# A gated recurrence and an FFT convolution: projecting all 256 channels at once, and shifts by half a period as signs in a second table

## The chip, the cores and the metric

One core of one Trainium2 chip runs the whole kernel. The metric is the time of one execution on the device in microseconds (us), as the median of several runs. One execution was also taken by the hardware profiler; all rows below come from that one.

## The reference

The input `x` has 4 batches of 6272 time steps and 256 channels. Two parts follow one another:

```python
sig = 1 / (1 + exp(-f_logit));  f = lower_bound + (1 - lower_bound) * sig
for t in range(S):                          # per batch and channel, S = 6272
    h = f[:, t] * h + (1 - f[:, t]) * x[:, t];  y[:, t] = h

x1, x2, x3 = split(y @ w_proj)              # 256 -> 3 * 256
X2 = rfft(x2, n=S, axis=1);  H = rfft(filter_fft, n=S, axis=0)
out = (x1 * irfft(X2 * H, n=S, axis=1) * x3) @ w_out
```

The convolution is circular over all 6272 steps, with one filter for each of the 256 channels.

## The kernel before

**The transform.** 6272 is 128 x 49, and these two have no common factor, so a transform of 6272 points becomes a transform of 128 points and one of 49, with no factors in between. Time index n is read as 128 q + 49 m, modulo 6272: for each of the 49 values of q (in the code `q_of(r)`), the 128 values of m are taken at a stride of 49 steps.

**The stages of a batch,** by the names in the code and the lines in the profile:

- `hgrn`: load `f_logit` and `x` in 13 pieces of 512 steps (`load`), sigmoid on ScalarE (`sig`, L353), the product on GpSimd (`u`, L355), transposes on TensorE (`sT` and `uT`, L362), the gate on ScalarE (`f`, L376) and the scan on VectorE (`scan`, L384). The scan writes h, in 16 bits, for two halves of 128 channels into the tile `HA`. For each piece GpSimd copies h once more past its end (`wrap`, L332), so that the stride of 49 can run over the end of the period: 100 copies in all.
- `phase_p` (`P`, L676): the projection to x2 and the gathering in one. The stationary operand is h at stride 49 (`HA[:, n0:n0 + Q * 127 + 1:Q]`), the moving operand 128 of the 256 columns of `W2`; two matmuls (the two halves of h's channels) for each r. It runs twice in a batch, for v = 0 and v = 1, since tile `X2` holds 128 channels; each time in 7 groups of 14 matmuls, and each group is copied out of PSUM into `X2` (`x2`, L327 on VectorE or L322 on ScalarE).
- `phase_f1` (`F1`, L690, evicted by `A`): the transform over 128 points, 8 pairs of channels in a unit, 16 units in a batch. `unit`: the transform over 49 points (`F2`, L738: four matmuls of 64 rows, two at a time in the upper and lower half of the array), the product with the filter's spectrum on VectorE (`prod`, L749), and the way back over 49 points (`I2`, L759, evicted by `Th`). `mini` (L711) and `zm` do the frequencies 0 and 64 of the 128 apart, with the filter's values in `Hm`.
- `gate`: x1 and x3 (`x13`, L412) are projected from h, evicted by ScalarE (`xs`, L424) and multiplied on GpSimd (`z`, L428) into `zt`.
- `phase_o`: the way back over 128 points (`I1`, L793), the product with `zt` (`y`, L799), the output projection (`proj`, L811), its eviction (`o`, L324) and the store.
- `prepare`, once: tables of sines, the weights, and the filter's spectrum (`rot`, `FF1`, `FF2`, L602, L619, L637), which goes to DRAM in 16 pieces (`hst`) and is loaded back in every batch (`H`).

**What sets the order.** The kernel records every operation with what it reads and writes. `Plan.schedule` then goes through a simulated time with costs for each operation, picks the next operation by start time and by priority (`LEAD` adds to priorities by kind and batch, `SHY` keeps kinds off engines), chooses the engine where there are two, and the PSUM banks (`room`: pairs of banks begin at an even bank). The instructions then stand on each engine in that order; on the chip an engine does not pass over an instruction that waits. Batches overlap: `hgrn` of the next batch runs beside the spectrum and the output stage of the present one. An operation of 64 rows (`ROWS`: F2, mini, I1, FF2, last) next to one of 128 rows makes TensorE change its mode.

**What waits for what around the change.** P needs all 26 pieces of h and all its copies past the end. The copies and the eviction buffer `A` of F1 lie in one part of `HA`. F1 needs all groups of `x2` of its half. P for v = 1 writes the same `X2` that F1 of v = 0 reads. `hgrn` of the next batch overwrites h, so it follows P for v = 1 and `x13`. Every `y` needs all 26 `z` of its batch.

Of the kernel before, what the change touches and what calls it, by code (L numbers as in the profile page):

```python
# [9 lines left out]
F32 = mybir.dt.float32  # L10
# [32 lines left out]
EW = 16384  # L43
AT = 6144
E0 = S - 176
E1 = S - 128


def q_of(r):

    return (18 * r) % Q
# [6 lines left out]
class Plan:  # L58
# [14 lines left out]
    SHY = {("A", "ACT"): 12, ("A", "DVE"): 31, ("Th", "ACT"): -13, ("Th", "DVE"): 637,  # L73
            ("afs", "ACT"): -3, ("afs", "DVE"): 28, ("f", "ACT"): -9, ("f", "DVE"): 18,
            ("f2", "ACT"): 978, ("f2", "DVE"): -356, ("fr", "ACT"): 65, ("fr", "DVE"): 449,
            ("fr", "POOL"): 310, ("hw", "ACT"): -51, ("hw", "DVE"): 109, ("o", "ACT"): -77,
            ("o", "DVE"): 1301, ("wrap", "ACT"): 636, ("wrap", "POOL"): 17, ("x2", "ACT"): 89,
            ("x2", "DVE"): 31}
# [6 lines left out]
        "A": (-75, 220, 598, 390), "F1": (561, 1834, 42, -2), "F2": (1153, -14, 2719, -82),  # L85
        "FF1": (861, 0, 0, 0), "FF2": (-3, 0, 0, 0), "H": (-41, -13, -344, -186),
        "I1": (-136, 778, -116, -26), "I2": (3, -264, 933, 15), "P": (1182, -300, 3, -112),
        "Th": (261, 84, -119, 0), "W": (3, 0, 0, 0), "f": (15, 14, 0, 0), "f2": (51, 0, 0, 0),
        "ff": (-67, 0, 0, 0), "fr": (1, 0, 0, 0), "hst": (146, 0, 0, 0), "hw": (622, 0, 0, 0),
        "last": (17, 0, 0, 0), "load": (-361, 63, 113, 165), "mini": (360, -626, -3, 39),  # L90
        "o": (-124, 109, 0, 37), "pre": (160, 0, 0, 0), "prod": (12, 0, -32, 135),
        "proj": (-1765, -5442, -1089, -504), "rot": (296, 0, 0, 0), "sT": (11, 7, 149, 755),
        "scan": (51, -58, -2, 148), "sig": (16, -225, 0, -421), "slot": (-4, 267, 15, 31),
        "store": (56, -11, -31, -3), "u": (12, -19, -7, -73), "uT": (1, -300, -798, -37),
        "warm": (-10, 0, 0, 0), "wrap": (505, -108, -107, -50), "x13": (0, -360, -13, -112),
        "x2": (1, 1, 50, 33), "xs": (251, 266, 157, 146), "y": (0, 101, -83, 11),
        "z": (-31, -259, -7, 5), "zm": (48, 300, -23, 414),
# [30 lines left out]
    @staticmethod  # L128
    def room(bank, n):

        best = None
        for b in range(0, 8, n):
            if None not in bank[b:b + n]:
                key = (max(bank[b:b + n]), n == 1 and bank[b ^ 1] is not None, b)
                if best is None or key < best:
                    best = key
        return best
# [108 lines left out]
def kernel(  # L246
# [24 lines left out]
    FT = konst.tile([128, 2, 128], F16, name="FT")  # L271
# [6 lines left out]
    Hm = konst.tile([128, 2, 2, 2, NEP], F16, name="Hm")  # L278


    HA = konst.tile([128, 2 * S + EW], F16, name="HA")
    A = HA[:, S + AT:S + AT + NA * UE * 128].rearrange("m (e r k) -> m e r k", r=2, k=64)
    HB = (0, S + EW)
# [4 lines left out]
    X2 = konst.tile([128, NEP // 2 * PW + 16], F16, name="X2")  # L288
# [16 lines left out]
    def E(a, z):  # L305

        return [("E", u) for u in range(a // 1024, (z - 1) // 1024 + 1)]
# [33 lines left out]
    def hgrn(b):  # L341
        for c in range(NCHK):
# [14 lines left out]
            for kh in range(2):  # L357
# [31 lines left out]
                a, o = (t0, t0) if kh == 0 else (max(t0, S - E1), EW - S + max(t0, S - E1))  # L389
                z = min(t0 + n, E0) if kh == 0 else t0 + n  # L390
                if z <= a:
                    continue
                op("wrap", {"POOL": 0.05 + (z - a) / 1015.0, "ACT": 0.08 + (z - a) / 1200.0},
                   lambda e, a=a, o=o, z=z, kh=kh: copy(
                       e, HA[:, S + o:S + o + z - a], HA[:, HB[kh] + a:HB[kh] + z]),
                   r=[("hn", kh, c)], w=E(o, o + z - a))
# [38 lines left out]
    def prepare(tmp):  # L435
        dve, pool, act = nc.vector, nc.gpsimd, nc.scalar
        at = (4096, 12288, 14336, 6144, 8192)
        raws = [(HA[:, S + a:S + a + 2048], E(a, a + 2048)) for a in at[:3]]
        raws += [(X2[:, i * 2048:(i + 1) * 2048], [("raw", i)]) for i in range(3)]
        raws += [(Hu[:, i].rearrange("m a e k -> m (a e k)"), [("Hu", i)]) for i in range(2)]  # L440
        raws += [(HA[:, S + a:S + a + 2048], E(a, a + 2048)) for a in at[3:]]
# [4 lines left out]
        def small(fn, n, r=(), w=(), e="DVE", k=1):  # L446
            op("pre", {e: k * (0.06 + n * (1.04e-3 if e == "DVE" else 1.5e-3))}, fn, r=r, w=w)

        op("pre", {"POOL": 1.0}, lambda e: make_identity(nc, iden), w=["iden"])
        rot = tmp.tile([128, 256], F32R, name="rot")  # L450
        for i in range(2):
            small(lambda e, i=i: dve.tensor_copy(rot[:, i * 128:(i + 1) * 128], iden[:]), 128,
                  r=["iden"], w=["rot"])
        op("pre", {"SP": 0.46}, lambda e: nc.sync.dma_start(
            wcol, lower_bound.rearrange("(a p) -> p a", p=128)), w=["wcol"], dma=0.3, lag=2.1)

        def oms(e):
# [4 lines left out]
        small(oms, 2, r=["wcol"], w=["om"], k=2)  # L462

        wp = HA[:, S:S + 3072].bitcast(F32).rearrange("p (k j) -> p k j", k=2)
        wo = HA[:, S + 3072:S + 4096].bitcast(F32).rearrange("p (k j) -> p k j", k=2)
        op("pre", {"SP": 0.46}, lambda e: nc.sync.dma_start(
            wp, moe_w_proj.rearrange("(a p) j -> p a j", p=128)), w=E(0, 3072), dma=2.1, lag=2.1)
        op("pre", {"SP": 0.46}, lambda e: nc.sync.dma_start(
            wo, moe_w_out.rearrange("(a p) j -> p a j", p=128)), w=E(3072, 4096), dma=0.8, lag=2.1)
        for kh in range(2):  # L470
# [4 lines left out]
               r=["om"] + E(0, 3072), w=["W13"])  # L475
            for p in range(2):
# [4 lines left out]
                   r=["om"] + E(0, 3072), w=["W2"])  # L481
        op("W", {"ACT": 0.5}, lambda e: act.copy(Wo[:], wo[:]), r=E(3072, 4096), w=["Wo"])


        scr, st = HA[:, S + 6144:S + 10240], E(6144, 10240)
# [5 lines left out]
        cols = tmp.tile([128, 9], F32, name="cols")  # L491
        kre, is0, kim, ore, oim, wt, k2, sgn, low = (cols[:, i:i + 1] for i in range(9))
        D1r = tmp.tile([128, 2, 128], F32R, name="D1r")
        FTr = tmp.tile([128, 2, TB], F32R, name="FTr")
# [4 lines left out]
        def iotas(e):  # L499
            pool.iota(pint, pattern=[[0, 1]], base=0, channel_multiplier=1)  # L500
            at = 0
            for n, pattern, base in (
                    (128, [[0, 2], [49, 64]], 0), (128, [[1568, 2], [0, 64]], 1568),
# [6 lines left out]
        small(iotas, 1260, r=["iden"], w=st + ["pint", "FT"], e="POOL")  # L510

        def args(e):
# [5 lines left out]
            stt(kim, in0=is0, scalar=64.0, in1=kre, op0=AOP.mult, op1=AOP.add)  # L518
# [19 lines left out]
            for i, (k, o) in enumerate(((kre, ore), (kim, oim))):  # L538
                ts(w[:, 520 + 256 * i:776 + 256 * i], in0=cI, scalar1=k, scalar2=o,
                   op0=AOP.mult, op1=AOP.add)  # L540

            big = 12582912.0
            ts(v, in0=w, scalar1=1.0 / S, scalar2=big, op0=AOP.mult, op1=AOP.add)
            ts(v, in0=v, scalar1=-big, scalar2=float(S), op0=AOP.add, op1=AOP.mult)
            dve.tensor_tensor(v, w, v, op=AOP.subtract)
        op("pre", {"DVE": 8.8}, args, r=st + ["pint", "rot"], w=["cols", "v"])
        op("pre", {"ACT": 0.97}, lambda e: act.activation(v, v, AF.Sin, scale=2.0 * math.pi / S),
# [3 lines left out]
            D1r[:], v[:, 0:128].unsqueeze(1).broadcast_to([128, 2, 128])), 256, r=["v"], w=["D1r"])  # L551
        for i in range(2):
            small(lambda e, i=i: dve.tensor_scalar(FTr[:, i], in0=tt[i], scalar1=low,
                                                   scalar2=None, op0=AOP.mult), 98, r=["v"],
                  w=["FTr"])

        def rest(e):
            pool.tensor_copy(D1[:], v[:, 0:128])
            for i in range(2):
                pool.tensor_scalar(FT[:, i, 0:98], in0=tt[i], scalar1=low, scalar2=None,  # L560
                                   op0=AOP.mult)
                pool.tensor_scalar(ID[:, i, :], in0=v[:, 520 + 256 * i:776 + 256 * i],
# [4 lines left out]
        op("pre", {"POOL": 3.9}, rest, r=["v", "FT"], w=["D1", "FT", "V", "ID"])  # L567
# [16 lines left out]
        small(gaps, 1920, r=["iden"], w=["f2e"], e="POOL")  # L584
# [3 lines left out]
        for g, r0 in enumerate(range(0, Q, 4)):  # L588
# [16 lines left out]
            for p in range(2):  # L605
# [4 lines left out]
                   w=[("f2", g, p)], src=rt)  # L610
        mX = tmp.tile([128, 2, NEP], F32R, name="mX")
        for u in range(NU):
            af = afs[:, u % 2]
            for h in range(2):
# [16 lines left out]
                w=["mX"], e="POOL")  # L631

            def second(e, pb, af=af):
                for r in range(2):
                    for e2 in range(2):
                        rows = slice(64 * e2, 64 * e2 + 64)
                        nc.tensor.matmul(PS[:TB, pb + e2, :], FTr[rows, r, :], af[rows, r],  # L637
# [11 lines left out]
        def last(e, pb):  # L649
            for k in range(2):  # L650
                for e2 in range(2):
                    rows = slice(64 * e2, 64 * e2 + 64)
                    nc.tensor.matmul(PS[:TB, pb + e2, k * NEP:(k + 1) * NEP], FTr[rows, k, :],
                                     mX[rows, k], start=True, stop=True)
        lst = op("last", {"PE": 0.3}, last, r=["mX", "FTr"], w=["FF2"], take=2)
        op("hw", either(512), lambda e, pb: copy(
            e, Hm[:TB, :, 0],
            PS[:TB, pb:pb + 2, 0:2 * NEP].rearrange("p a (k i) -> p a k i", k=2), HS),
           w=["Hm"], src=lst)
        for h in range(2):  # L660
            op("hst", {"SP": 0.36}, lambda e, h=h: nc.sync.dma_start(
# [226 lines left out]
```

## Time and profile before

| what | value |
|---|---|
| median of 3 runs | 520.24 us (518.5 to 520.66) |
| the profiled execution | 522.43 us, span of its instructions 520.6 us |
| clock granted to TensorE, mean | 0.984 |
| busy: TensorE, VectorE, ScalarE, GpSimd | 490.2, 440.3, 401.5, 394.5 us |
| DMA traffic | 116.53 MB |

PE is TensorE's matmuls, PEld its weight loads, DVE VectorE, ACT ScalarE, POOL GpSimd and SP the engine that issues the transfers. A busy time counts the union of an engine's instructions. Matmuls are pipelined: the mean duration of one is far longer than the time from the start of one to the start of the next, and the latter, called its pace below, is what a stream of them costs.

### The profile page before, as it was taken

What the parts mean: (1) busy time and instruction counts of PE and PEld (TensorE: products, weight loads), DVE (VectorE), ACT (ScalarE), POOL (GpSimd) and SP (SyncE); (2) the same over time, 40 slices, a digit from 0 to 9 for tenths busy, and PEclk for the clock granted to TensorE, in tenths of its full rate; (3) what the DMA queues carried; (4) which work ended last, traced back from release to release, by engine and by line L of the source; (5) the groups of instructions that cost most, each with busy time, mean ns of one, the idle gap of its engine ahead of it and who ended that gap; (6) DMA issues with size and microseconds to landing.
All of it is one profiled execution on the core that took longest, in us unless ns stands there. A gap on an engine that the chain in (4) does not pass through costs nothing.

```text
span 520.6 us, 13604 instructions
## 1 busy us (share of the span) xinstructions
PE 490.2 (94%) x5389; PEld 373.9 (72%) x5389; DVE 440.3 (85%) x464; ACT 401.5 (77%) x584; POOL 394.5 (76%) x363
## 2 busy tenths in 40 slices
PE   6989999999998999999999989999999999999796
PEld 5867777676655889687666879586677886585485
DVE  6899776898989798898998888998988998789764
ACT  5879797759986875768997864969998856869644
POOL 3576786949997987948999884949999957968800
PEclk9899999999998999999999999999999999999989
DMA  8978899434679899344879896444688951433157
GB/s 310 407 284 255 287 333 317 152 103 133 210 228 262 258 342 336 138 144 121 286 223 254 300 312 219 132 142 129 207 285 283 391 213 71 135 98 98 59 208 289
DMA packets 41938, 116.53 MB, mean 224 GB/s; under 512 B 4398, under 2 KB 6514, under 8 KB 41874
## 3 DMA queue, kind: packets, MB, share of 16 engines
q1 hardware_dynamic: 41874, 115.66, 65.7%
q8 instruction: 42, 0.69, 0.5%
q14 instruction: 22, 0.18, 0.1%
HBM read 84.54 MB, written 31.00 MB: 222 GB/s over the span
## 4 chain that ended last, share of the span: by engine, by line
PE 62%; DMA 15%; POOL 8%; ACT 7%; issue 3%; DVE 2%; SPq 0%; POOLq 0%; ACTq 0%; DVEq 0%
PE PS L412 13%; PE PS L362 11%; PE PS L676 9%; PE PS L811 8%; PE PS L759 7%; DMA FL<-in_f_logit_dram 6%; PE PS L738 5%; POOL zt L428 5%; PE PS L690 4%; DMA H<-Hu 4%; PE PS L793 4%; DMA XT<-in_x_dram 2%; POOL XT L355 2%; DMA HA<-in_moe_filter_fft_dram 2%; PE PS L619 1%
## 5 line engine op out<-in xcount | busy, mean ns | idle before, releaser
L428 POOL TENSOR_TENSOR zt<-x1s,x3s 128x490 f16<-128x490 f32 (+1 forms) x104 | 201.2, 1952 | 46.3 <-ACT x3s L424 34.3
L749 DVE TENSOR_TENSOR PP<-PS,Hu 98x1008 f16<-98x1008 f32 x128 | 146.6, 1198 | 13.1 <-PE PS L738 6.4
L355 POOL TENSOR_TENSOR XT<-XT,FL 128x1024 f32<-128x1024 f32 (+1 forms) x52 | 117.4, 2258 | 25.4 <-DMA XT<-in_x_dram 10.7
L384 DVE TENSOR_TENSOR_SCAN HA<-fTs,HA,PS 128x512 f16<-128x512 f32 (+1 forms) x96 | 113.9, 1204 | 14.2 <-PE PS L362 12.4
L412 PE MATMUL PS<-HA,W 128*128 128x490 f16 (+1 forms) x416 | 105.3, 370 | 3.4 <-ACT x1s L424 2.0
L324 ACT ACTIVATE osb<-PS 128x1024 f32<-128x1024 f32 (+1 forms) x52 | 50.7, 976 | 34.9 <-PE PS L811 33.8
L799 DVE TENSOR_TENSOR ys<-PS,zt 128x1024 fp32r<-128x1024 f32 (+1 forms) x52 | 59.9, 1156 | 20.0 <-PE PS L793 12.3
L376 ACT ACTIVATE fTs<-PS,nomc 128x512 f32<-128x512 f32 (+1 forms) x97 | 64.6, 667 | 11.8 <-PE PS L362 10.0
L424 ACT ACTIVATE x1s<-PS 128x490 f32<-128x490 f32 (+1 forms) x104 | 60.8, 585 | 12.3 <-POOL zt L428 7.6
L424 ACT ACTIVATE x3s<-PS 128x490 f32<-128x490 f32 (+1 forms) x104 | 61.1, 587 | 10.5 <-PE PS L412 10.4
L353 ACT ACTIVATE FL<-FL 128x1024 f32<-128x1024 f32 (+1 forms) x52 | 52.8, 1016 | 18.8 <-DMA FL<-in_f_logit_dram 18.8
L811 PE MATMUL PS<-Wo,ys 128*128 128x256 f32 x392 | 61.3, 299 | 4.3 <-DVE ys L799 2.2
L362 PE MATMUL PS<-iden,XT 128*128 128x128 f32 x392 | 62.2, 279 | 2.5 <-POOL XT L355 1.7
L362 PE MATMUL PS<-iden,FL 128*128 128x128 f32 x392 | 61.2, 277 | 2.8 <-ACT Th L322 2.4
L412 PEld LDWEIGHTS <-W 128*128 128x128 f16 x416 | 34.7, 98 | 39.9 <-issue 19.1
L332 POOL COPY HA<-HA 128x512 f16<-128x512 f16 (+2 forms) x100 | 56.2, 602 | 7.5 <-DVE HA L384 7.4
L759 PEld LDWEIGHTS <-PP 98*128 98x128 f16 x1024 | 50.4, 98 | 11.1 <-issue 3.6
L322 ACT CAST Th<-PS 128x784 f16<-128x784 f32 x64 | 52.8, 826 | 7.1 <-PE PS L759 6.9
L811 PEld LDWEIGHTS PS<-Wo,ys 128*128 128x128 f32 x392 | 51.7, 195 | 7.9 <-ACT osb L324 2.8
L759 PE MATMUL PS<-VA,PP 98*128 98x98 f16 x512 | 52.9, 208 | 2.2 <-POOL PP L741 1.2
L327 DVE CAST X<-PS 128x896 f16<-128x896 f32 x49 | 50.2, 1090 | 4.8 <-PE PS L676 4.6
L676 PEld LDWEIGHTS <-HA 128*128 128x128 f16 x784 | 52.6, 152 | 1.9 <-issue 0.6
(90 smaller groups left out, 694.1 us busy)
## 6 DMA issues: line engine op xcount, KB each, us to landing
Hu<-H SPq DMA_DIRECT2D x64, 392.0 KB
FL<-in_f_logit_dram SPq DMA_DIRECT2D x48, 512.0 KB
XT<-in_x_dram SPq DMA_DIRECT2D x48, 512.0 KB
out_dram<-osb SPq DMA_DIRECT2D x48, 512.0 KB
HA<-in_moe_filter_fft_dram SPq DMA_DIRECT2D x7, 512.0 KB
H<-Hu SPq DMA_DIRECT2D x16, 196.0 KB
H<-Hu SPq DMA_DIRECT2D x16, 128.0 KB
X<-in_moe_filter_fft_dram SPq DMA_DIRECT2D x3, 512.0 KB
```

The lines of the kernel that those rows point to most:

```text
L355: op("u", {"POOL": 0.1 + 0.553 * nb}, lambda e, xt=xt, ft=ft: nc.gpsimd.tensor_tensor(xt, xt, ft, op=AOP.mult), r=[("ft", k)], w=[("xt", k)])
L362: nc.tensor.transpose(PS[:, p, j:128 * nb:nb], src[:, j, cols], iden[:])
L376: nc.scalar.activation(fT, PS[:, p, 0:n], AF.Identity, scale=by, bias=1.0)
L384: nc.vector.tensor_tensor_scan(h, fT, PS[:, p, 0:n], init, op0=AOP.mult, op1=AOP.add),
L412: nc.tensor.matmul(PS[:, p, 0:n], W13[:, kh, js], HA[:, HB[kh] + t0:HB[kh] + t0 + n], start=(kh == 0), stop=(kh == 1))
L424: nc.scalar.activation(xs(i), PS[:, p, 0:n], AF.Copy, scale=1.0 if i else ZS),
L428: nc.gpsimd.tensor_tensor(late["zt"][:, jb, :, m0:m0 + nm], xs(0).rearrange("p (m r) -> p r m", r=Q), xs(1).rearrange("p (m r) -> p r m", ...
L676: nc.tensor.matmul(pp[:, r - 7 * g, :], HA[:, n0:n0 + Q * 127 + 1:Q], W2[:, kh, v * 128:v * 128 + 128], start=(kh == 0), stop=(kh == 1))
L749: nc.vector.tensor_tensor(PP[:TB, k, o, :, :, 1:64], px.unsqueeze(1).broadcast_to([TB, 2, UE, 63]), hh[:, :, :, 1:64], op=AOP.mult)
L759: nc.tensor.matmul(PS[:, ib + o, pr * TB:(pr + 1) * TB], PP[:TB, k, o, n, 2 * pr:2 * pr + 2, :], v[:TB], start=(n == 0), stop=(n == 1))
L799: nc.vector.tensor_tensor(late["ys"][:, yk, :, 0:rn * 128], PS[:, cb:cb + 2, 0:rn * 128], late["zt"][:].rearrange("p k r m -> p k (r m)") ...
L811: nc.tensor.matmul(po[:, i, :], late["ys"][:, yk, kh, i * 128:(i + 1) * 128], Wo[:, kh, :], start=(kh == 0), stop=(kh == 1))
```

## The change

1. `phase_p` runs once in a batch. Each matmul moves all 256 columns of `W2`; there are 98 in a batch in place of 196, in 13 groups. `X2` holds 256 channels.
2. Where q is over 24, the stationary operand starts half a period earlier (`- S // 2`). It then holds the same 128 values rotated by 64, and a rotation by half of 128 points changes only the sign of the odd frequencies. So `FT` gets a second table with these signs, F1's columns (`D1`) are ordered into 32 even and 32 odd frequencies, and each matmul of F2 becomes two of half its columns, one with each table: 8 matmuls of 256 columns in place of 4 of 512. `ID` follows the new order.
3. h is copied past its end for 3072 steps in both channel halves: 48 copies in place of 100. The copies and `A` have places of their own in `HA`.
4. `Hm` moves into the unused columns of `X2`; its second, rotated copy comes from four more small matmuls (`last`) in place of two transfers.
5. `room` lets pairs of banks begin at any bank. `LEAD` and `SHY` have other values, the kinds of `prepare` are told apart, and so the whole order is another.

```diff
-        for b in range(0, 8, n):
+        for b in range(9 - n):
...
-    HA = konst.tile([128, 2 * S + EW], F16, name="HA")
+    HA = konst.tile([128, 2 * (S + WR) + AW], F16, name="HA")
...
-    X2 = konst.tile([128, NEP // 2 * PW + 16], F16, name="X2")
+    X2 = konst.tile([128, NEP * PW + 16], F16, name="X2")
+    xv = X2[:, 0:NEP * PW].rearrange("m (i c) -> m i c", c=PW)
+    Hm = xv[:, :, Q:Q + 8].rearrange("m i (e a k) -> m e a k i", e=2, a=2)
...
-                a, o = (t0, t0) if kh == 0 else (max(t0, S - E1), EW - S + max(t0, S - E1))
-                z = min(t0 + n, E0) if kh == 0 else t0 + n
-                if z <= a:
+                z = min(t0 + n, WR)
+                if z <= t0:
                     continue
...
-                    (128, [[0, 2], [49, 64]], 0), (128, [[1568, 2], [0, 64]], 1568),
+                    (128, [[0, 2], [49, 2], [98, 32]], 0), (128, [[1568, 2], [0, 64]], 1568),
...
+                pool.tensor_scalar(FT[:, 1, i, 0:98], in0=FT[:, 0, i, 0:98], scalar1=odd,
+                                   scalar2=None, op0=AOP.mult)
...
-    def phase_p(b, v):
+    def column(t, q):
+        n0 = t + 128 * q - (S // 2 if q > Q // 2 else 0)
+        return HA[:, n0:n0 + Q * 127 + 1:Q]
+
+    def phase_p(b):
-        for g in range(7):
+        for g, r0 in enumerate(range(0, Q, 4)):
+            rn = min(4, Q - r0)
...
-                        n0 = HB[kh] + 128 * q_of(r) - (S if kh and r else 0)
-                        nc.tensor.matmul(pp[:, r - 7 * g, :], HA[:, n0:n0 + Q * 127 + 1:Q],
-                                         W2[:, kh, v * 128:v * 128 + 128],
+                        nc.tensor.matmul(pp[:, r - r0, :], column(HB[kh], q_of(r)), W2[:, kh, :],
                                          start=(kh == 0), stop=(kh == 1))
-            pp = op("P", {"PE": 0.902}, mm, r=hn + E(0, AT) + E(AT + 4096, EW), take=2)
-            op("x2", either(896, 1.2), lambda e, pb, g=g: copy(
+            pp = op("P", {"PE": 0.005 + 0.214 * rn}, mm, r=hn + Wr(0) + Wr(1) + ["W2"], take=2)
+            op("x2", either(256 * rn, 1.2), lambda e, pb, r0=r0, rn=rn: copy(
...
-            for r in range(2):
-                for e2 in range(2):
-                    rows = slice(64 * e2, 64 * e2 + 64)
-                    nc.tensor.matmul(PS[:, xb + e2, :], FT[rows, r, :], A[rows, ka:ka + UE, r, :],
-                                     start=(r == 0), stop=(r == 1))
+            for o in range(2):
+                ks = slice(32 * o, 32 * o + 32)
+                for r in range(2):
+                    for e2 in range(2):
+                        rows = slice(64 * e2, 64 * e2 + 64)
+                        nc.tensor.matmul(
+                            PS[:, xb + e2, :].rearrange("p (i k) -> p i k", k=64)[:, :, ks],
+                            FT[rows, o, r, :], A[rows, ka:ka + UE, r, ks],
+                            start=(r == 0), stop=(r == 1))
...
-        for v in range(2):
-            phase_p(b, v)
-            for q in range(2 * v, 2 * v + 2):
+        phase_p(b)
+        for q in range(NU // NA):
...
```

## The prediction

> **What bounds the kernel now.** I read the page first: the busy times, then the chain that ended last.
>
> ```profile
> PE 490.2 (94%) x5389; PEld 373.9 (72%) x5389; DVE 440.3 (85%) x464; ACT 401.5 (77%) x584; POOL 394.5 (76%) x363
> PE 62%; DMA 15%; POOL 8%; ACT 7%; issue 3%; DVE 2%; SPq 0%; POOLq 0%; ACTq 0%; DVEq 0%
> PE PS L412 13%; PE PS L362 11%; PE PS L676 9%; PE PS L811 8%; PE PS L759 7%; DMA FL<-in_f_logit_dram 6%; PE PS L738 5%; POOL zt L428 5%; PE PS L690 4%; DMA H<-Hu 4%; PE PS L793 4%; DMA XT<-in_x_dram 2%; POOL XT L355 2%; DMA HA<-in_moe_filter_fft_dram 2%; PE PS L619 1%
> ```
>
> TensorE is the bound: 94% busy and 62% of the chain, with the projection P (L676) at 9% of the span, some 47 us. Then I cut the span where each batch's P begins (87.5, 202.1, 314.1 and 425.4 us); the columns are the length, then busy time and count of PE, PEld, DVE, ACT and POOL, granted clock, DMA share and GB/s.
>
> ```profile
> 0.00:87.50 87.50, 78.70 (x577) 62.86 (x578) 69.53 (x104) 69.57 (x94) 57.61 (x82) 0.98 0.88 314
> 87.50:202.10 114.60, 109.19 (x1250) 82.51 (x1249) 100.19 (x97) 90.78 (x136) 95.13 (x79) 0.99 0.69 222
> 202.10:314.10 112.00, 106.17 (x1221) 81.62 (x1220) 98.50 (x96) 88.20 (x132) 95.43 (x82) 0.98 0.71 228
> 314.10:425.40 111.30, 109.33 (x1286) 83.98 (x1284) 101.00 (x98) 89.33 (x133) 93.45 (x79) 1.00 0.64 221
> 425.40:520.60 95.20, 86.86 (x1066) 62.94 (x1064) 71.11 (x72) 63.58 (x93) 52.84 (x42) 0.97 0.40 142
> ```
>
> The first stage is loads (DMA 0.88). In the middle three TensorE is at 95 to 98%, but VectorE has 100 and GpSimd 95 of 112 us: little room for any engine to be late. Durations by form come next.
>
> ```profile
> L676 PE MATMUL PS<-W,HA 128*128 128x128 f16 x784 | 53.4, 228 | 0.0
> L676 PEld LDWEIGHTS <-HA 128*128 128x128 f16 x784 | 52.6, 152 | 1.9 <-issue 0.6
> L738 PEld LDWEIGHTS <-FT 64*128 64x128 f16 x256 | 8.1, 94 | 14.0 <-issue 10.4
> L332 POOL COPY HA<-HA 128x512 f16<-128x512 f16 x88 | 51.3, 621 | 4.0 <-DVE HA L384 3.9
> ```
>
> P never waits (0.0), so its own pace is its price. Paces come from the timeline: start, length and count of a run of matmuls.
>
> ```profile
> 16.72 2.36 PE L573 MATMUL PS<-iden 128*128 128x256 f16 x20
> 189.11 0.63 PE L793 MATMUL PS<-ID,Th 64*128 64x128 f16 x16
> 202.19 6.59 PE L676 MATMUL PS<-W,HA 128*128 128x128 f16 x98
> 203.41 7.11 DVE L327 CAST X<-PS 128x896 f16<-128x896 f32 x7 [1.17 <-PE PS L676]
> 227.97 0.60 PE L738 MATMUL PS<-HA,FT 64*128 64x512 f16 x4
> 228.50 0.59 PE L412 MATMUL PS<-HA,W 128*128 128x490 f16 x2
> ```
>
> Last, the chain where the last batch turns to its output:
>
> ```profile
> 486.82 0.87 PE PS L412 x4
> 488.09 3.47 POOL zt L428 x2
> 491.56 1.53 POOLq L883
> 493.12 1.24 DVE ys L799
> ```
>
> TensorE's last `x13` is followed by two `z` on GpSimd, and all `y` wait for those.
>
> **The change, part by part.** Pace = (length − duration of one) / (count − 1).
>
> P: 128 columns go at (6.59 − 0.228)/97 = 0.0656 us, so 784 cost 51.4 us. The same form with 256 columns is in the warming matmuls at the start: (2.36 − 0.273)/19 = 0.110 us, where 0.273 is L573's mean duration. 392 x 0.110 = 43.1 us: 8.3 us less. The strided load of h lasts 152 ns, but streams at 0.0656 now, so under 0.110 it is hidden; if a load held the stream for all of its 152 ns, the pace would be 0.152 and P would lose, but today's pace excludes that. Of P's 51.4 us some 47 are on the chain (0.92), so I count **−7.6**. The Trainium skill, "TensorE: Matmul & The Clock Gate", section "Back-to-back issue gap", gives streams of loads and matmuls about 81 ns at 128 columns and 131 ns at 512; my estimate between them is 98 ns at 256, and P would go from 63.5 to 38.3 us, 25 us less. The trace has neither end of it (65.6 ns, and 0.44 us for two of 490 columns), so the trace's paces stand.
>
> F2: today four matmuls in two pairs hold TensorE for 2 x 0.22 us, since the two of a pair start together. After, four pairs of 256 columns. The nearest row with a load for every matmul is I1: 16 of 64 rows and 128 columns in 0.63 us, (0.63 − 0.22)/15 = 0.027 each, or 0.055 to 0.057 a pair. Twice that for 256 columns is 0.114, four pairs 0.456 in place of 0.44: 64 units x 0.016 = **+1.0**. At the other end the added loads (94 ns) are not hidden: two more in each half of the array, 0.19 us a unit and 12.0 us in all, or 24.1 us if the halves take turns. No row suggests a gain. I take the I1 row, which has the same shape of load and hides it at half the columns. Against this stands a rule of the same page, Part 3, section "The mechanism": a weight load overlaps running matmuls only if its row group differs; by it my estimate is the 12.0 us. But I1 loads before each matmul, at 95 ns a load, and keeps 57 ns a pair.
>
> Changes of mode: between F2's start and the next kind lie 0.53 us, of which 0.44 is its own, so 0.09 a change. In the new order I count 258 changes where there are 278: 20 x 0.09 = 1.8 us, at TensorE's 62% of the chain **−1.1** (0 to −1.8). The four more `last` matmuls and `Hm`'s two lost transfers lie in the first stage, which the loads hold: 0.
>
> x2: VectorE gets 40 copies of 1024 elements and 4 of 256 for 49 of 896, ScalarE 8 for 7. Back to back, 896 take 7.11/7 = 1.016 us; by two evictions of F1 in 2.35 us 1024 take 1.175. So 48.6 us for 49.8, nothing gained. But F1 now waits for all 13 groups: VectorE's 11 end 1.17 + 10 x 1.175 + 0.4 = 13.3 us after P's start, P itself after 98 x 0.110 = 10.8. Of these 2.5 us the order covers 1.8 in the first batch (the filter's last units, four `x13` matmuls), 2.8 in the second (two groups of `proj` and I1), 2.5 in the others (twelve `x13`). I take 0.5 a batch for what is not covered: **+2.0**; 0 if all is, +10.0 if the cover fails. Today's tails cost nothing (no wait of L690 for it on TensorE's list), so nothing is won. `x2` also holds VectorE for 12 us; queued behind are scans and `prod`, and its other work changes by −2 us in all (18 evictions of F1 to 15, 15 of the filter's `afs` to 21, 7 gates to 3).
>
> Copies past the end: 52 fewer, 56.2 us to 48 x 0.59 = 28.3. None is on the chain; `z` and `u` behind them in GpSimd's queue are. GpSimd's 8% of the chain are 41.6 us; if they shrink as its work does (28/394), that is 3.0. I take **−1.0** (0 to −3.0). `pad`'s memset doubles (1 us), in the load-bound stage: 0.
>
> End: in the new order five I2 and three F2 stand between the last `x13` and I1, today one I2. With 0.69 us for an I2 (the chain has it at 481.0 us) that is 4 x 0.69 + 3 x 0.44 = 4.1 us more TensorE work beside the last `z`, so the wait of 488.1 to 493.1 us mostly closes. TensorE's own gaps there are 0.5, 1.3 and 1.8 us. I take **−2.0** (0 to −3.6), as `prod` on VectorE is late next.
>
> Sum: −7.6 + 1.0 − 1.1 + 2.0 − 1.0 − 2.0 = **−8.7 us**. The profiled execution took 522.43 us (span 520.6 and 1.8 around it), so it would take 513.7; it stood 2.2 above the median, and the median goes from 520.24 to **511.5 us**.
>
> **The rivals.** (a) All favourable ends: −8.3 − 1.8 − 3.0 − 3.6 = −16.7 us, 503.5 us. For it speak the full engines of the middle stages, where less GpSimd work loosens the rest; against it, that copies are off the chain. (b) The gain turns into a wait: P at one stretch shuts TensorE for `x13` and transposes for 10.8 us, and F1 behind it waits for `x2`. With the cover gone (10.0 for 2.0) the sum is −0.7: 519.5 us, no change. For it speaks VectorE at 100 of 112 us; against it the `x13` that stand there. (c) Slower: F2's added loads are exposed, in all 64 units. It decides from (8.7 + 1.0)/64 = 0.15 us a unit; at 0.19 to 0.38 the sum is +2.3 to +14.4 us, in the middle 528.6 us. For it speaks that pieces of 32 columns are in no row of this size; against it I1. (d) That it does not do what it says can be left out: the built order has 392 matmuls of 256 columns and 48 copies.
>
> **How the numbers follow.** Forecast 0.52, (a) 0.20, (b) 0.16, (c) 0.12. About 0.5% (2.6 us) is what a measurement of this kernel can tell from no change: 517.6 to 522.8. The forecast and (a) are faster, with a quarter of (b): 0.76. The rest of (b) is the same: 0.12. (c) is slower: 0.12. The range goes from the favourable ends, 503.5, to 521.0, past (b): that leaves (c) and a little of (a) out. The forecast's own range is 506.5 to 516.5.
>
> **What would show it.** P (128x256) at a pace of 0.110 us and 43 us in all; F2's eight in about 0.65 us from first start to last end, against 0.60 now; copies past the end at 28 us; no gap over 1 us on TensorE between P and F1; the last `z` over before I1 of the last batch starts. Wrong would be: F2 over 0.75 us, F1 waiting for X by 2 us a batch, or VectorE's share rising to TensorE's.

## The result and the profile after

The changed kernel takes 538.65 us (535.68 to 541.41) where the kernel before takes 520.45: 1.034 times as long, 95% interval 1.025 to 1.043. A gain of 8.7 us was forecast; it lost 18.2. (520.45 is the median of four runs, 520.24 above that of the first three.) Medians count every run; ratios and intervals leave out the few runs in a slower state. The profiled execution has a span of 539.1 us against 520.6. The page, busy times and the chain by engine:

```profile
PE 493.9 (92%) x5257; PEld 385.5 (72%) x5257; DVE 451.1 (84%) x465; ACT 410.2 (76%) x586; POOL 370.1 (69%) x315
PE 27%; DVE 10%; ACT 7%; POOL 7%; issue 4%; DMA 3%; ACTq 0%; DVEq 0%; POOLq 0%; SPq 0%
```

TensorE's share of the chain fell from 62 to 27% (the chain is not followed back to the start, its shares add up to 58%), while that of VectorE rose from 2 to 10. GpSimd has 24 us less to do, VectorE 11 more. The stages, cut where P begins as before (length, then PE, PEld, DVE, ACT and POOL busy, clock, DMA share, GB/s):

```profile
0.00:82.90 82.90, 75.99 (x565) 62.09 (x566) 72.45 (x116) 65.73 (x86) 52.41 (x72) 0.98 0.90 317
82.90:198.40 115.50, 106.71 (x1164) 82.84 (x1165) 99.38 (x92) 95.96 (x139) 94.33 (x71) 0.97 0.69 229
198.40:325.40 127.00, 117.88 (x1316) 92.08 (x1308) 103.41 (x95) 97.32 (x143) 88.04 (x68) 0.99 0.64 214
325.40:438.80 113.40, 106.72 (x1211) 83.39 (x1212) 102.20 (x95) 88.79 (x131) 84.83 (x66) 1.00 0.64 213
438.80:539.10 100.30, 86.56 (x1011) 65.06 (x1009) 73.65 (x69) 62.42 (x91) 50.53 (x41) 0.94 0.35 124
```

The first stage is 4.6 us shorter, the third 15 longer (it also holds 95 more matmuls, so part of that is work that moved), the last 5. To see whether TensorE has less to do, one can multiply each form's pace in the trace by its count (0.0648 and 0.109 us a matmul for P before and after, 0.112 and 0.0566 for F2, 0.207 for a full `x13`, 0.109 for a transpose and so on) and add 0.09 us for each of the 278 and 258 changes of mode. This is an estimate, good to 2 or 3 us; differences between kernels are better than that, since most terms are the same:

| kernel | TensorE's own work, us | rest of the span, us | of it between P's start and F1's, four batches |
|---|---|---|---|
| before | 465 | 55 | 1.4 |
| changed | 456 | 83 | 14.1 |

So the work did shrink, by 9.3 us. The rest, time in which TensorE was late or its clock low, grew by 27.8: 12.7 of it lie behind P, some 7 more in the last stage, the others are spread. Groups of the changed kernel by form (busy us, mean ns of one, idle before):

```profile
L703 PE MATMUL PS<-W,HA 128*128 128x256 f16 x392 | 45.5, 273 | 4.0 <-DVE HA L395 1.8 <-DVE X L338 1.7 <-ACT Hu L335 0.5
L338 DVE CAST X<-PS 128x1024 f16<-128x1024 f32 x40 | 55.2, 1481 | 3.3 <-PE PS L703 2.2 <-DMA H<-Hu 1.1
L338 DVE CAST X<-PS 128x256 f16<-128x256 f32 x4 | 5.2, 1312 | 0.0
L333 ACT CAST X<-PS 128x1024 f16<-128x1024 f32 x8 | 11.9, 1483 | 12.0 <-PE PS L703 12.0
L335 ACT ACTIVATE X<-PS 98x1024 f16<-98x1024 f32 x1 | 4.8, 4810 | 1.4 <-PE PS L680 1.4
```

The evictions of x2 take 1481 and 1483 ns for 1024 elements, and those of 256 elements almost as long, 1312. `Hm`, whose elements now stand alone 226 bytes apart, takes 4810 ns. And the timeline of the last batch's P (start, length):

```profile
439.84 8.95 PE L703 MATMUL PS<-W,HA 128*128 128x256 f16 x79 [0.54 <-DVE HA L395]
440.86 14.57 DVE L338 CAST X<-PS 128x1024 f16<-128x1024 f32 x11 [1.08 <-PE PS L703]
449.08 2.12 PE L703 MATMUL PS<-W,HA 128*128 128x256 f16 x18 [0.29 <-DVE X L338]
451.70 0.99 PE L422 MATMUL PS<-HA,W 128*128 128x490 f16 x4 [0.50 <-DVE X L338]
455.49 0.68 PE L716 MATMUL PS<-D,X 128*128 128x128 f16 x9 [0.66 <-DVE X L338]
```

P itself runs at its pace, (8.95 − 0.27)/78 = 0.111 us, until PSUM is full of groups that VectorE has not evicted. Then P, the `x13` behind it, and F1 all wait for X.

### The profile page after: what moved, and what is told of

It is laid out like the page before. It is cut to its first block, busy times and chain, and to the rows that moved or that the text cites. A ratio compares the mean times of both kernels' runs of the same rounds, so it can differ in the third digit from the quotient of the medians.

```text
span 539.1 us, 13270 instructions
## 1 busy us (share of the span) xinstructions
PE 493.9 (92%) x5257; PEld 385.5 (72%) x5257; DVE 451.1 (84%) x465; ACT 410.2 (76%) x586; POOL 370.1 (69%) x315
## 4 chain that ended last, share of the span: by engine, by line
PE 27%; DVE 10%; ACT 7%; POOL 7%; issue 4%; DMA 3%; ACTq 0%; DVEq 0%; POOLq 0%; SPq 0%
PE PS L835 6%; PE PS L373 6%; POOL zt L438 5%; DVE X L338 5%; PE PS L422 5%; PE PS L817 3%; PE PS L784 3%; DVE PP L774 3%; PE PS L761 3%; PE PS L716 2%; ACT HA L333 1%; DMA FL<-in_f_logit_dram 1%; ACT x3s L434 1%; ACT Th L333 1%; DVE HA L395 1%
## 5 line engine op out<-in xcount | busy, mean ns | idle before, releaser
L438 POOL TENSOR_TENSOR zt<-x1s,x3s 128x490 f16<-128x490 f32 (+1 forms) x104 | 200.5, 1949 | 69.2 <-DVE ys L823 38.7
L422 PE MATMUL PS<-HA,W 128*128 128x490 f16 (+1 forms) x416 | 104.2, 369 | 2.6 <-DVE X L338 1.8
L387 ACT ACTIVATE fTs<-PS,nomc 128x512 f32<-128x512 f32 (+1 forms) x101 | 68.4, 681 | 15.6 <-PE PS L373 14.3
L333 ACT CAST Th<-PS 128x784 f16<-128x784 f32 x64 | 53.4, 840 | 12.9 <-PE PS L784 12.7
L338 DVE CAST X<-PS 128x1024 f16<-128x1024 f32 (+1 forms) x44 | 58.4, 1466 | 3.3 <-PE PS L703 2.2
L422 PEld LDWEIGHTS <-W 128*128 128x128 f16 x416 | 36.6, 98 | 33.3 <-issue 11.0
L373 PEld LDWEIGHTS PS<-iden,XT 128*128 128x128 f32 x392 | 44.9, 142 | 15.5 <-issue 3.9
L333 ACT CAST HA<-PS 128x1024 f16<-128x1024 f32 x49 | 50.3, 1033 | 6.8 <-PE PS L716 6.3
```

Source lines behind the costliest of these rows:

```text
L333: nc.scalar.copy(dst, src)
L338: nc.vector.tensor_copy(dst, src)
L373: nc.tensor.transpose(PS[:, p, j:128 * nb:nb], src[:, j, cols], iden[:])
L387: nc.scalar.activation(fT, PS[:, p, 0:n], AF.Identity, scale=by, bias=1.0)
L422: nc.tensor.matmul(PS[:, p, 0:n], W13[:, kh, js], HA[:, HB[kh] + t0:HB[kh] + t0 + n], start=(kh == 0), stop=(kh == 1))
L438: nc.gpsimd.tensor_tensor(late["zt"][:, jb, :, m0:m0 + nm], xs(0).rearrange("p (m r) -> p r m", r=Q), xs(1).rearrange("p (m r) -> p r m", ...
```

## The experiments

Two theories. **1:** the slow evictions are the loss. **2:** the new order is the loss, whatever the evictions cost; the priorities and the plan's costs decide where every instruction of every engine stands, and also which engine takes an eviction that two can do. "Order" means both below.

**Three edits that were planned anew.** e1 moves 128 columns at a time again:

```diff
-            pp = op("P", {"PE": 0.005 + 0.214 * rn}, mm, ...)       # 13 groups, 256 columns
+        for v in range(2):                                         # 2 x 7 groups, 128 columns
+                pp = op("P", {"PE": 0.902}, mm, ...)
```

> The changed kernel, but P moves 128 of the 256 columns at a time again (196 matmuls of 128 columns for each of two channel halves, both before F1, groups of 7 r, evicted in 896 elements as in the kernel before); signs, F2 in eight, 48 copies past the end, and the plan's costs for P and x2 go with it, so the order is planned anew. Theory 1 (the evictions of x2 in runs of 4 elements are the loss: 1.33 us each back to back in place of 1.16, 0.92 for the last one, 4.8 us for Hm): x2 back at 1.02 us for 896, and although P costs 8 us more on TensorE the time falls from 538.7 to 522 to 528 us. Theory 2 (the new order and the new priorities are the loss, whatever the evictions cost): 534 us or more.

e2 aligns the pairs of channels in X2:

```diff
-    X2 = konst.tile([128, NEP * PW + 16], F16, name="X2")     # 113 columns a pair
+    X2 = konst.tile([128, NEP * XW + 12], F16, name="X2")     # 116
```

> The changed kernel with 116 in place of 113 columns for a pair of channels in X2, so that every run of 4 elements that x2 writes begins at a multiple of 8 bytes; the added columns are zeroed. If the evictions are slow because half of the runs begin at odd 2-byte places: x2 on VectorE falls from 1.33 to about 1.16 us back to back, and theory 1 then has 522 to 530 us. If they are slow because the runs are short, x2 stays at 1.33 and the time within 1% of 538.7. Theory 2: 534 us or more even if x2 gets faster.

e3 puts the pairs innermost:

```diff
-    xv = X2[:, 0:NEP * PW].rearrange("m (i c) -> m i c", c=PW)
+    xc = XC[:, 0:NEP * 128].rearrange("m (c i) -> m c i", i=NEP)
```

> The changed kernel with X2 laid out the other way: the 128 pairs of channels innermost, so x2 writes runs of 128 elements, and Hm too; F1 loads its weights at a stride of 256 bytes. Theory 1: x2 at 1.16 us on VectorE and 1.03 on ScalarE, Hm at about 1.0 us; F1's pace goes from 0.056 to about 0.065 us as P's strided loads had (4.6 us more on TensorE); 518 to 526 us. Theory 2: 534 us or more.

Measured: 599.05, 601.44 and 636.80 us, ratios of 1.15 to 1.23. All expectations were missed by far, for a reason outside the edits: each changed a cost or added an operation in the plan, and the order came out anew with priorities that did not fit. VectorE's busy tenths in 40 slices, from the page of e2, show a stretch in which it stands almost still:

```profile
DVE  7987845799999979875596000999968975894054
```

For e2 that is shown by e5 below, the same edit with the order kept, 69 us faster; for e1 and e3 it is argued from that, and e3 has a slower F1 besides (512 matmuls at 0.07 us more are 36 us of TensorE). As times the three tell only that an order cost e2 69 us. Their rows are still good. With 116 columns (e2), and for e3 the weight loads and matmuls of F1:

```profile
L339 DVE CAST X<-PS 128x1024 f16<-128x1024 f32 x40 | 46.8, 1221 | 6.0 <-PE PS L706 6.0
L334 ACT CAST X<-PS 128x1024 f16<-128x1024 f32 x8 | 8.1, 1011 | 12.0 <-PE PS L706 12.0
L339 DVE CAST X<-PS 128x256 f16<-128x256 f32 x4 | 5.2, 1288 | 0.0
```

```profile
L716 PE MATMUL PS<-D,XC 128*128 128x128 f16 x512 | 72.2, 285 | 3.8 <-ACT HA L335 1.3 <-ACT osb L337 0.6 <-ACT fTs L389 0.4
L716 PEld LDWEIGHTS <-XC 128*128 128x128 f16 x512 | 70.0, 259 | 9.5 <-issue 7.1 <-ACT XC L335 0.2
```

Alignment to 8 bytes alone brings the evictions from 1481 to 1221 ns on VectorE and from 1483 to 1011 on ScalarE, as fast as those of F1 into `A` (1215 and 1019 before). So it is where the runs start, not their length of 4. At 226 bytes a pair, every second pair starts at an odd multiple of 2 bytes and only every fourth at a multiple of 8; which of the two has the price, no run tells. Single elements stay slow (1288). e3's way has fast evictions throughout (1217 and 1012 ns, 414 for 256 elements, 1018 for `Hm`), but F1's loads at a stride of 256 bytes take 259 ns, and its matmuls a median of 0.126 us from start to start in place of 0.056.

**e4: the plan is told what the evictions took.** Same operations, other costs in the plan (`...` marks what is left out):

```diff
-            op("x2", either(256 * rn, 1.2), ...
+            op("x2", {"ACT": 0.36 + 0.28 * rn, "DVE": 0.78 + 0.138 * rn}, ...
```

and 4.8 for `Hm`.

> The changed kernel, same instructions, but the plan is told what the evictions of x2 took (1.33 us on VectorE, 1.48 on ScalarE, 0.92 for the last; 4.8 for Hm), so the order is planned anew around them. Theory 1 (the work itself is the loss): little comes back, 532 to 538 us. If the loss is mostly that the order was planned for shorter evictions: 522 to 530 us.

Measured 524.70 us, ratio 1.013 (1.008 to 1.018), well clear of the changed kernel's 1.034. The evictions are as slow as ever:

```profile
L338 DVE CAST X<-PS 128x1024 f16<-128x1024 f32 x37 | 51.2, 1480 | 2.8 <-PE PS L703 2.8
```

By the ratios 11 us (0.0216 x 520), by the medians 14, came back from the order alone, three more of these evictions on ScalarE included. Theory 1 did not allow that.

**e5 and e6: fast evictions, order kept.** After e1 to e3 I held the plan's operations and costs fixed, so that each engine has the same list of instructions, one memset at the start apart, and changed only the width to 116.

> Every instruction of the changed kernel in the same order on its engine, with one memset of zeros added on GpSimd at the start; X2 has 116 columns for a pair, so x2 copies of 1024 elements take 1.22 instead of 1.48 us (mean) on VectorE and 1.01 instead of 1.48 on ScalarE, as the earlier run with 116 columns had. This takes the price of the odd alignment away and leaves the order. Theory 1 (slow evictions are the loss of 18 us): 520 to 526 us. Theory 2 (the order is the loss): 533 us or more. Half and half: 527 to 532 us.

> The order of the run whose plan was told the slow evictions (524.7 us), with X2 at 116 columns a pair, so the evictions are now faster than planned. If evictions still stand on the path in that order: 515 to 521 us, faster than or equal to the kernel before. If that order hides them already: 523 to 526 us.

e5: 531.96 us, at the slow end of "half and half"; ratio 1.029 (1.022 to 1.037), by the ratios 2.7 us less than the changed kernel, by the medians 6.7, and the intervals overlap. The traces are clearer. The stretch behind P is where it shows: 7.9 us late in four batches, not 14.1. In the second batch VectorE's eleven evictions, the changed kernel first, then e5:

```profile
199.93 14.53 DVE L338 CAST X<-PS 128x1024 f16<-128x1024 f32 x11
```

```profile
198.88 12.60 DVE L339 CAST X<-PS 128x1024 f16<-128x1024 f32 x11
```

e6: 524.25 us, 1.012 (1.007 to 1.017), the same as e4. In the order that was planned for slow evictions, shortening them brings nothing. So the price of the misplaced runs of 4 is a seventh of the loss by the ratios and a little over a third by the medians (the intervals reach from nothing to about half), and that in the order of the changed kernel alone. (`Hm` and the single elements stay slow in e5, 4683 and 1298 ns; e8 below has all of the slow evictions.)

**e7 to e10: orders of equal effort.** I let a search change LEAD and SHY at random for about two million orders each, judged by the plan, for the kernel before (e7), the changed kernel with the costs of e4 (e8) and the one with 116 columns (e9). e10 changes one cost of the kernel before, P's 0.902 to 0.918.

> The kernel before, same operations, with priorities from a search of about two million orders in its own plan (random steps in LEAD and SHY, started from its values). Theory 2 (the order decides): faster than before by 1 to 6 us, 513 to 518 us. If its order was already as good as an order gets on the chip: 517 to 521 us.

> The changed kernel, same operations, whose plan knows what x2 and Hm took (1.33 and 4.8 us), with priorities from a search of the same length. Theory 2: most of the loss goes, 515 to 522 us, and what is left against the searched kernel before is the price of the change itself; with the PE work 9 us less and the evictions 13 us more I expect the two within 1%. Theory 1: 525 us or more.

> The changed kernel with X2 at 116 columns a pair and the plan's costs for the evictions as measured there, priorities from a search of the same length. If the change is good once the evictions are fast and the order fits: 508 to 515 us, faster than the searched kernel before. If the 9 us of TensorE work do not reach the end in any order that the plan finds: within 1% of it.

> The kernel before, same operations and same priorities, with one cost in the plan changed: P's 14 matmuls at 0.918 us, as measured, in place of 0.902. The order comes out anew. Theory 2: the priorities fit one set of costs alone, so even this costs 3 to 12 us (523 to 532 us). If orders of equal priorities are about equal: 519 to 522 us.

| kernel | median, us | ratio to before (95%) |
|---|---|---|
| e7 before, searched | 512.58 | 0.988 (0.982 to 0.994) |
| e8 changed, searched | 510.57 | 0.984 (0.979 to 0.990) |
| e9 changed, 116 columns, searched | 517.20 | 0.994 (0.990 to 0.998) |
| e10 before, one cost changed | 522.23 | 1.008 (1.003 to 1.012) |

e7 and e8 came out faster than either of their expectations; e9 missed its first range and stands within 1% of e7, its second; e10 lies between its two. e8 has the work of the changed kernel, slow evictions included (1488 ns), and takes 28 us less by the medians, 26 by the ratios. Its stages:

```profile
0.00:83.30 83.30, 75.86 (x569) 61.73 (x569) 68.24 (x108) 69.77 (x95) 50.62 (x71) 0.98 0.89 315
83.30:197.10 113.80, 110.40 (x1247) 85.84 (x1244) 103.43 (x96) 99.13 (x141) 92.31 (x70) 1.00 0.71 240
197.10:302.90 105.80, 103.71 (x1204) 81.64 (x1202) 101.22 (x94) 89.46 (x132) 87.14 (x67) 1.00 0.72 235
302.90:407.80 104.90, 100.67 (x1157) 79.30 (x1158) 95.82 (x91) 87.48 (x131) 86.02 (x66) 1.00 0.66 218
407.80:506.00 98.20, 89.27 (x1098) 67.76 (x1092) 78.78 (x73) 66.54 (x97) 53.47 (x42) 0.97 0.43 154
```

The middle stages are 105 to 114 us long where the changed kernel has 113 to 127, with VectorE at 91 to 96%. TensorE's own work in e8 is 457 us, the rest of the span 49. Theory 2 stands: the order is the main loss. What in the order does it is open: e7's search, for one, also moved 23 of the evictions of x2 from VectorE to ScalarE. Between e7 (whose plan keeps its own costs) and e8, at equal effort, the change is worth 0.4%, and the intervals overlap. e9 should have been the best and was not. Its order is a worse one (61 us beside TensorE's own work, in a trace 2.3 us above its median, where e8 has 49); why its search ended there is not shown, so it says nothing of 116 columns. e10 moved the time by 4 us by the ratio, at the low end of what theory 2 had.

**e11 and e12: two prices in the order of e8,** which is kept on every engine. e11 splits each of P's matmuls into two of 128 columns, as before the change:

```diff
-                        nc.tensor.matmul(pp[:, r - r0, :], column(...), W2[:, kh, :], ...)
+                        for cs in (slice(0, 128), slice(128, 256)):  # each with both kh
+                            nc.tensor.matmul(pp[:, r - r0, cs], column(...), W2[:, kh, cs], ...)
```

> The searched changed kernel (510.6 us), same order on every engine, but each of P's matmuls of 256 columns is two of 128, as the kernel before has them: 784 at 0.0656 us for 392 at 0.110, 8.3 us more on TensorE and nothing else. If TensorE's time reaches the end as the prediction had it (0.92): 518 us. If it is absorbed where P waits for the evictions anyway (P took 11 to 13 us a batch where its pace asks for 10.8, and the evictions end later still): 511 to 514 us.

> The searched changed kernel, same order on every engine, one memset more at the start, X2 at 116 columns a pair: the evictions take 1.22 and 1.01 us in place of 1.48 and the order does not know it. If the evictions stand on the path as they did in the order of the changed kernel (6.7 us of 18): 503 to 507 us, the fastest version. If a fitting order hides them, as the order of the told plan did: 509 to 512 us.

e11: 516.73 us, ratio 0.996 (0.992 to 1.000), against e8's 0.984: 6.2 us more for 8.3 us of TensorE, nearer to the first expectation. e12: 508.20 us, ratio 0.978 (0.973 to 0.983), the fastest version, between its two expectations and 3 us under e8 by the ratios, with overlapping intervals. It is 2.2% faster than the kernel before; how much of that is the order can be read from e7, 1.2%.

## Why the prediction was wrong, point by point

**P: right.** 0.0656 to 0.110 us a matmul was forecast, with 0.92 of the 8.3 us reaching the end. The pace came out at 0.109 (median from start to start), and e11 shows 6.2 of 8.3, or 0.75, reaching the end once the order fits; the intervals allow 2.6 to 9.8 us, so the 0.92 too. (The 0.273 us in the working was L573's median duration; its mean is 0.308, which would have given 0.108.)

**F2: right within 1 us, rival (c) refuted.** 0.65 us for the eight was forecast; the trace has 0.61. The next kind starts 0.543 us after F2 (median), where it was 0.538 before, so the occupancy is 0.45 us and grew by 0.005 where I had 0.016:

```profile
466.36 0.61 PE L761 MATMUL PS<-HA,FT 64*128 64x256 f16 x8
```

The second load in each half of the array is hidden. The rule of the Trainium skill that would expose it ("TensorE: Matmul & The Clock Gate", section "The mechanism", a load overlaps only if its row group differs) does not describe these loads. The same section names a background weight buffer as a second way to overlap; no run here tells whether that is it.

**Mode changes and copies past the end: work right, worth not shown.** There are 258 changes in the trace, and the copies cost 27.8 us (forecast 28.3). No run prices either alone. What GpSimd saved became waiting. Idle time of L438, `z`, by what ended it, changed kernel:

```profile
  DVE ys L823: 38.7, 3
  ACT x3s L434: 30.3, 15
```

Before, the first was 11.6 us. `z` may not overwrite `zt` until the last `y` of the batch before has read it, so a GpSimd with less to do waits for VectorE.

**x2: the term that was mis-sized.** I priced 1024 elements at 1.175 us and the last 256 at 0.4 from the evictions of F1 and had VectorE end 13.3 us after P's start, for +2.0 us. Back to back it took 1.33 and 0.92; F1 began 16.2 to 17.7 us after P, and the stretch lost 14.1 − 1.4 = 12.7 us, more than the +10.0 at my far end. In the first batch F1 also waited 2.3 us for `Hm`, which I had counted at 0: its eviction stands behind P (96.0 to 100.8 us), not in the first stage. With fast evictions in the same order (e5) the 14.1 become 7.9, of which 4.6 are in the first batch, where `Hm` is as slow as ever. e8 still has 7.2 there, e12 6.0 and e9 3.8, where e7 has 0.6. So part of this wait stayed in every order with P in one stretch that was run, with fast evictions too. The row I took writes contiguously. The nearest row in kind, 896 elements in runs of 7, showed no penalty on VectorE, so nothing in the trace of before gave 1.33; but ScalarE's row for the same copies (1098 ns for 896, where 1024 contiguous ones take 1019) did show that such runs can cost, and I passed over it. The Trainium skill ("SBUF — State Buffer", section "Operand start alignment") lets an operand of 2-byte data start at any multiple of 2 bytes, and says that this is about legality, not speed; what these runs add is a price for where the runs inside the operand start. Rival (b) had named this place, at 0.16.

**The end of the last batch: the wait closed and another took its place.** The last `z` ended at 501.8 us, before I1 (509.1), as forecast. But TensorE now waited there for `prod`, named in the forecast as late next, without a price. Then its clock fell (start, length, of runs of matmuls):

```profile
506.40 0.20 PE L784 MATMUL PS<-VA,PP 98*128 98x98 f16 x1 [0.69 <-DVE PP L774]
511.53 2.08 PE L835 MATMUL PS<-Wo,ys 128*128 128x256 f32 x8 [0.54 <-DVE ys L823]
519.31 1.21 PE L835 MATMUL PS<-Wo,ys 128*128 128x256 f32 x8
```

The same eight matmuls take 2.08 us at half the clock and 1.21 after. The records have half clock from 507.5 us for 10.2 us, where the kernel before has 3.4 at this place. At most 3.4 us of the loss is this (half of the difference of 6.8). By the working of the table above, the rest of the whole last stage grew from 13 to 23 us, 3 of them behind P, where −2.0 had been forecast.

**The order: the step that failed.** The sum took the kernel before's lost time as it was and corrected it in four places. I wrote that the whole order is another, and priced it only by mode changes, by what stands between P and F1, and at the end. By the ratios e4 and e8 show the order to be worth 11 us and then 15 more, more than every term of the sum; a search of the same length won 6 us in the kernel before too (e7). Rows of before said which way it leaned: the middle stages had TensorE's own work plus 5.5 to 11.0 us each, so a better order had 27 us there to win at the most, and nothing bounded what a poorer one could lose. It needed a term with a large upper end, and a rival on the slower side for it. The rival on that side, (c), stood on F2 and was wrong.

## What to carry to other kernels

Where a planner writes the order, an edit and its order are two changes: compare them with the list of instructions kept, and then with each list searched for equally long, with the durations of a trace as its costs. When an engine's work is cut in a kernel whose engines are all nearly full, ask first which eviction must now keep up with it, and take its price from a row with the same pattern of writes.

## What the runs showed of the hardware that was not expected

- 16-bit runs of 4 elements from PSUM: 1221 ns on VectorE and 1011 on ScalarE for 1024 when all start at multiples of 8 bytes, 1481 and 1483 when the pairs stand 226 bytes apart. Runs of one element are slow either way: 1288 to 1312 ns for 256 on VectorE, and 4.7 ns each for `Hm`'s 1024 on ScalarE.
- Strided weight loads (94 to 101 ns when contiguous): 142 ns at a stride of 98 bytes, hidden under 256 columns; 259 ns at 256 bytes, where the pace of 128-column matmuls went from 0.056 to 0.126 us.
- Not settled: why the nearest orders differ so much on the chip. No run moved single instructions; e4 and e8 exchange the whole list.
